# A tuned attention and adapter kernel with another beginning: bias factors made from the bias rows, products of zeros, and two stores on ScalarE's queue

## The chip, the core and the metric

The kernel runs on one core of a Trainium2 chip. The core has five engines with queues of their own: TensorE (PE; its weight loads are listed as PEld), VectorE (DVE), ScalarE (ACT), GpSimd (POOL) and SyncE (SP), which here only issues transfers. ScalarE can issue transfers too. Sixteen DMA engines carry the transfers of all queues. The metric is the device time of one execution in microseconds (us); lower is better.

## The reference: what is computed

The first half is attention with a relative position bias, for 8 batch entries, 8 heads, 576 positions and a head size of 64. The second half takes the attention output as 4608 rows of 512 and adds a mixture of 8 adapters of rank 16, of which each row uses the best two.

```
scores = q k^T / 8 + bias_table[bucket(|i - j|)]        (32 buckets)
attn   = softmax(scores);  x = attn v                   (rows: 4608 x 512)
logits = x w_gate;  the two best experts, weights w by softmax
out    = x + sum over the two of w * ((x A[e]) B[e])
```

From a distance of 128 on all positions share the last bucket. A constant in the scores drops out of the softmax, so the kernel subtracts that last bucket from the table, and the bias is zero outside a band of 128 positions on both sides.

## The kernel before, in words

**Units.** The work is cut into 32 units: a batch entry and a pair of heads (`hp`, 4 per entry). Of the 576 positions the first 512 are the main part and the last 64 the tail. A unit's main scores are computed in four groups of keys (`keys`, L416), each for 2 heads and 512 queries, and ScalarE takes the exponential of each group out of PSUM (L431, 128x1024). `edges` (L481) computes main keys against tail queries and tail keys against main queries, with one exponential (L494, 128x1024), and `corners` and `corners_first` compute tail against tail. `values` (L540) multiplies the probabilities by the values, and `normalise` divides. The second half of the kernel (gates, adapters, output) runs some units behind, spread over the same loop.

**The order of the work.** Nothing is scheduled automatically: each engine's queue runs in the order in which the code is written. Per unit `u` the loop (from L775) issues the loads of unit `u + 4` (L781), the edges, two groups of keys, the first half of the values of unit `u - 1`, two groups of keys, a turn (transposes by TensorE and a copy by VectorE, L354) that brings the q and k of unit `u + 2` into the layout that the scores need, and the second half of the values. Some turns also take the tail of a batch entry (`tl_item`, L385): that of entry 2 in unit 5. POOL casts q, k, v and the tails to bf16 a unit or two ahead (`prep`, `prep_late`), and the adapter weights in unit 4 (`weights_cast`, L273). There are three PSUM buffers for scores, used in turn, and two for everything small.

**Loads.** Nearly all transfers are issued by SP in one order, and eight may be under way: each waits for the one eight places before it, besides the cast that frees its buffer. The loads of q, k, v of unit 3 follow the start's own (L667 on); the tail's q and k are one 64-row transfer each (`load_tail`, L116), which for entry 0 are already split into two pairs of heads and two pairs of heads (L163 and L658). The loads of unit 6, the adapter weights and the tail of entry 1's values follow in unit 2 of the loop, the tail of entry 2 in unit 3.

**The bias in the main scores.** The 8 rows of the bias by distance, `gx`, are put in two interleaved halves into `gp` (L194, L195), written to a DRAM scratch `gd` (L651), and read back so that each of 64 partitions gets the row shifted by one (`table`, L205): `Wt`. A product with a reversed identity then adds the band to the scores in PSUM (L427). `Wt` comes in four transfers: for each head of the pairs, the first two pairs of heads (L206) and later the last two.

**The bias on the edges and corners** is a factor on the probabilities instead. ScalarE takes the exponential of the rows (`ge`, L655), mirrored by VectorE first (L654); the result goes to a second scratch (L657) and comes back shifted as `Wn` (`table_n`, L209, two transfers). 48 small products (`factors_l`, L216) and 16 more (`factors_t`, L236) turn pieces of it into the factors `EL`, `EC` and `ET`, and VectorE and POOL multiply the edge probabilities by them (`edge_l`, L496; `edge_t`, L501; `corners_bias`, L476).

**Products of zeros.** `keep_busy(n)` (L643) issues `n` products of 128x128 by 128x512 zeros into a PSUM buffer that nobody reads. Before, there is one call with 9, ahead of the first turn (L678).

**The end.** The last nine tiles of output rows are finished by TensorE and copied out of PSUM by ScalarE or VectorE (`out_x`, L835); each copy is followed by its store, on SP's queue. A main tile is one store of 256 KB (L309), a tail tile two of 128 KB (L331).

Of the kernel before, what the change touches and what calls it, by code (L numbers as in the profile page):

```python
# [38 lines left out]
def kernel(  # L39
# [11 lines left out]
    nc = tc.nc  # L51
# [123 lines left out]
    gp = cp.tile([H, 2, GP], BF16, tag="gp")  # L175
    nc.vector.memset(gp, 0.0)
    nc.vector.memset(tvs[0], 0.0)
    for i in range(2):
        nc.gpsimd.memset(pcs[i], 0.0)
    bts = cp.tile([H, NB], FP32, tag="bts")  # L180
# [22 lines left out]
    ET = cp.tile([128, HP, 2, 128], BF16, tag="ET")  # L203

    def table(h, g0, g1, eng):  # L205
        eng.dma_start(out=Wt[h * 64:h * 64 + 64, g0:g1, :WN],  # L206
                      in_=_dram(gd, (2 * g0 + h) * 2 * GP, [[1, 64], [4 * GP, g1 - g0], [1, WN]]))

    def table_n(h, eng):  # L209
        eng.dma_start(out=Wn[h * 64:h * 64 + 64, :, :193],  # L210
                      in_=_dram(gnd, h * GL + C - 127, [[2, 64], [2 * GL, HP], [1, 193]]))
# [4 lines left out]
    def factors_l():  # L216
        n = HP * 64
        ps = [mp.tile([128, 512], FP32, name="fl", tag="mm") for _ in range(2)]
        for hp in range(HP):
            for e in range(2):  # L220
                for h in range(2):
                    rows = slice(h * 64, h * 64 + 64)
                    for f in range(2):
                        nc.tensor.matmul(ps[h][f * 64:f * 64 + 64, hp * 64 + e * 32:hp * 64 + e * 32 + 32],
                                         lhsT=Wn[rows, hp, 129 - e:193 - e],
# [3 lines left out]
                                     lhsT=Wn[rows, hp, 1 - e:65 - e], rhs=turned(h)[:, :32],  # L229
# [6 lines left out]
    def factors_t():  # L236
        ps = [mp.tile([128, 512], FP32, name="ft", tag="mm") for _ in range(2)]
        for hp in range(HP):
            for e in range(2):
                for h in range(2):  # L240
                    rows = slice(h * 64, h * 64 + 64)
                    o = (2 * hp + e) * 64
                    nc.tensor.matmul(ps[h][64:, o:o + 64], lhsT=turned(h), rhs=Wn[rows, hp, 129 - e:193 - e],
# [4 lines left out]
    def presets():  # L248
        nc.gpsimd.memset(tvs[1], 0.0)
# [44 lines left out]
    def main_tile(b, j, f):  # L294
# [13 lines left out]
        def store(ot):  # L308
            nc.sync.dma_start(out=out[b * S:b * S + SM, :].rearrange("(p c) n -> p c n", c=4)[:, j + 2 * f, :],  # L309
                              in_=ot)  # L310
# [3 lines left out]
    def tail_tile(b):  # L314
# [14 lines left out]
        def store(ot, engs=(nc.sync, nc.sync)):  # L329
            for o in range(2):  # L330
                engs[o].dma_start(out=out[(b - 1 + o) * S + SM:(b + o) * S, :],  # L331
                                  in_=ot[64 * o:64 * o + 64, :])
# [321 lines left out]
    nc.vector.tensor_copy(gx[:, C - FAR + 1:C], _ap(gx, C + FAR - 1, [[-1, FAR - 1]]))  # L654
    nc.scalar.activation(ge[:, 128:448], gx[:, 128:448], ACT.Exp, scale=scale)  # L655
# [383 lines left out]
```

## Time and profile before

| what | value |
|---|---|
| median of 3 runs | 196.99 us (196.67 to 197.87) |
| the profiled execution | 198.93 us, of which the profile's span is 197.0 us |
| TensorE busy | 178.4 us (91% of the span) |
| ScalarE busy | 165.6 us (84%) |
| VectorE, POOL busy | 134.6 us (68%), 120.9 us (61%) |
| moved by DMA | 40.65 MB, 206 GB/s over the span |

The span is what the trace covers, from its first to its last event; all positions in time below count from its start. The profile was taken of one execution, which took 198.93 us; the median of the runs without it is 196.99. A row of a timeline reads: start, length, engine, line, operation, output<-inputs, shape, count, and in brackets how long the engine stood idle before and what released it. SPq and ACTq rows are the issuing of transfers, not the transfers themselves. A row that merges several instructions ("x4") gives the stretch from the first start to the last end.

### The profile page before, as it was taken

How to read it: one execution, taken by the hardware profiler on the slowest of the kernel's cores; microseconds unless marked ns; L12 is line 12 of the kernel's file. 1: busy time of each engine (PE TensorE's matmuls, PEld its weight loads, DVE VectorE, ACT ScalarE, POOL GpSimd, SP SyncE). 2: the span in 40 equal slices, each digit the busy share in tenths (PEclk: the TensorE clock that was granted, in tenths of full speed). 3: DMA queues.
4: the chain of work that ended last, by engine and by line, in shares of the span. 5: the costliest groups of instructions: out<-in, count | busy, mean ns of one | idle time of the engine just before them, and what ended most of it. 6: DMA issues, size and time to landing. Idle time of an engine off the chain costs nothing.

```text
span 197.0 us, 9952 instructions
## 1 busy us (share of the span) xinstructions
PE 178.4 (91%) x4272; PEld 130.2 (66%) x4272; DVE 134.6 (68%) x340; ACT 165.6 (84%) x210; POOL 120.9 (61%) x292
## 2 busy tenths in 40 slices
PE   7497998986999999999999999998999999999860
PEld 2244666664777777777677777775777777788740
DVE  6644564454467777777877768778777787788760
ACT  3459679974899999999999999998999999999670
POOL 5543656496394959495949586776859493734410
PEclk9958699997899999999999999999999999999996
DMA  5757978998977788978888967887879851114066
GB/s 137 230 149 198 277 192 239 233 208 248 269 179 227 240 235 231 283 248 216 206 253 261 275 150 219 257 269 166 236 217 315 245 180 57 57 58 108 5 242 237
DMA packets 68483, 40.65 MB, mean 206 GB/s; under 512 B 22216, under 2 KB 63704, under 8 KB 68440
## 3 DMA queue, kind: packets, MB, share of 16 engines
q1 hardware_dynamic: 67896, 39.76, 71.4%
q8 instruction: 33, 0.54, 1.3%
q10 hardware_dynamic: 544, 0.26, 0.5%
q14 instruction: 10, 0.08, 0.2%
HBM read 30.56 MB, written 9.45 MB: 203 GB/s over the span
## 4 chain that ended last, share of the span: by engine, by line
PE 52%; ACT 18%; DMA 10%; issue 6%; DVE 5%; SPq 4%; POOL 1%; POOLq 0%; ACTq 0%
ACT pk L431 14%; PE pv L518 11%; PE tx L370 8%; PE sc L422 6%; PE sc L427 4%; PE sc L492 3%; PE sc L489 3%; ACT pt L494 3%; DMA Bf<-in_moe_B_dram 3%; DMA qkt<-in_k_dram 3%; PE pv L535 2%; PE pv L526 2%; PE pv L565 2%; PE dl L614 2%; DMA vs<-in_v_dram 2%
## 5 line engine op out<-in xcount | busy, mean ns | idle before, releaser
L431 ACT ACTIVATE pk<-sc 128x1024 bf16<-128x1024 f32 x120 | 113.9, 1033 | 6.1 <-PE sc L427 6.1
L422 PE MATMUL sc<-tx 64*64 64x512 bf16 x480 | 50.5, 400 | 0.0
L427 PE MATMUL sc<-Wt,anti 64*64 64x256 bf16 (+1 forms) x480 | 43.4, 317 | 0.4 <-DMA Wt<-g_d 0.3
L518 PEld LDWEIGHTS <-pk 128*128 128x128 bf16 x1024 | 38.0, 98 | 8.5 <-issue 1.7
L518 PE MATMUL pv<-v,pk 128*128 128x65 bf16 x992 | 42.1, 195 | 0.7 <-DVE xn L558 0.7
L372 DVE COPY tx<-tx 128x2048 bf16<-128x2048 bf16 (+7 forms) x35 | 35.2, 1007 | 9.4 <-PE tx L370 7.4
L494 ACT ACTIVATE pt<-sc 128x1024 bf16<-128x1024 f32 x32 | 32.8, 1025 | 8.4 <-PE sc L492 6.4
L558 DVE TENSOR_TENSOR xn<-pv,rc 128x320 bf16<-128x320 f32 x62 | 30.5, 492 | 2.1
L581 POOL TENSOR_TENSOR a<-z,top 128x16 f32<-128x16 f32 (+2 forms) x15 | 3.3, 221 | 39.1 <-DVE top L571 37.2
L557 DVE RECIPROCAL rc<-pv 128x5 f32<-128x5 f32 x62 | 11.9, 193 | 21.5 <-PE pv L565 13.0
L303 DVE TENSOR_TENSOR ot<-dl,xn 128x512 f32<-128x512 f32 x24 | 16.6, 690 | 11.0 <-PE dl L614 11.0
L422 PEld LDWEIGHTS <-tx 64*64 64x64 bf16 x480 | 16.1, 108 | 10.2 <-issue 1.6
L136 POOL CAST v<-vs 128x512 bf16<-128x512 f32 x32 | 20.1, 629 | 3.7 <-DMA vs<-in_v_dram 3.0
L140 POOL CAST qn<-qs 128x512 bf16<-128x512 f32 x29 | 17.7, 610 | 3.9 <-DMA qs<-in_q_dram 3.5
L427 PEld LDWEIGHTS <-anti 64*64 64x64 bf16 x480 | 18.6, 109 | 1.3 <-issue 1.1
L140 POOL CAST kn<-ks 128x512 bf16<-128x512 f32 x29 | 17.8, 613 | 0.8 <-DMA ks<-in_k_dram 0.8
L535 PE MATMUL pv<-v,pt 128*128 128x65 bf16 x248 | 17.8, 195 | 0.0
L526 PE MATMUL pv<-vb,pt 128*128 128x130 bf16 x124 | 17.6, 225 | 0.0
L499 POOL TENSOR_TENSOR pt<-pt,EL 128x128 bf16<-128x128 bf16 x32 | 13.8, 430 | 5.9 <-ACT pk L431 5.9
L370 PEld LDWEIGHTS <-qn 64*128 64x128 bf16 x256 | 7.5, 95 | 12.0 <-issue 5.4
L535 PEld LDWEIGHTS <-pt 128*128 128x128 bf16 x256 | 14.2, 99 | 0.0
L504 DVE TENSOR_TENSOR pt<-pt,ET 128x256 bf16<-128x256 bf16 x32 | 12.5, 394 | 0.1
(141 smaller groups left out, 304.0 us busy)
## 6 DMA issues: line engine op xcount, KB each, us to landing
qs<-in_q_dram SPq DMA_DIRECT2D x32, 256.0 KB, 4.3
vs<-in_v_dram SPq DMA_DIRECT2D x64, 128.0 KB, 3.9
out_dram<-ot SPq DMA_DIRECT2D x32, 256.0 KB, 3.7
ks<-in_k_dram SPq DMA_DIRECT2D x62, 128.0 KB, 4.1
vt<-in_v_dram SPq DMA_DIRECT2D x16, 128.0 KB, 4.6
out_dram<-ot SPq DMA_DIRECT2D x8, 128.0 KB, 2.8
qkt<-in_q_dram SPq DMA_DIRECT2D x7, 128.0 KB, 5.3
qkt<-in_k_dram SPq DMA_DIRECT2D x7, 128.0 KB, 5.3
```

Source lines behind the costliest of these rows:

```text
L136: eng.tensor_copy(t[:, :, :, :D].rearrange("p c h d -> p h c d"), s)
L140: copy(t.rearrange("p c h d -> p h c d"), s)
L370: nc.tensor.transpose(ps[:, a, cols], src(i, a), ident[rows, rows])
L372: copy(sb[:, :n], ps.rearrange("p a (c i) -> p c a i", i=64)[:, :n])
L422: nc.tensor.matmul(sc[prt, h, :], lhsT=kT[rows, c * 128 + f * 64:c * 128 + f * 64 + 64], rhs=qT[rows, :], start=True, stop=False, skip_gro ...
L427: nc.tensor.matmul(_ap(sc[prt, h, :], p0, [[256, 2], [128, 2], [1, n]]), lhsT=turned(h), rhs=_ap(Wt[rows, hp, :], 2 * y0 + (GP if e else 1 ...
L431: nc.scalar.activation(probs[u][0][:, c, :, :], sc, ACT.Exp, scale=scale)
L494: nc.scalar.activation(probs[u][1][:, 64:], sc.rearrange("p h x -> p (h x)"), ACT.Exp, scale=scale)
L518: nc.tensor.matmul(pv[:, o:o + W1], lhsT=pk_slice(u, c, h, j + 2 * f), rhs=vm[:, c, h, :], start=first, stop=False, skip_group_check=True)
L526: nc.tensor.matmul(_ap(pv, h * W1, [[130, 2], [1, W1]]), lhsT=probs[u][1][:, x0:x0 + 128], rhs=tvs[b % 2][:, 2 * hp + h].rearrange("p f d ...
L535: nc.tensor.matmul(pv[:, o:o + W1], lhsT=probs[u][1][:, x0:x0 + 128], rhs=vts[u % NV][:, c, h, :], start=False, stop=False, skip_group_che ...
L558: nc.vector.tensor_tensor(xs[b][:, j, hp], _ap(pv, 0, [[W1, 5], [1, D]]), _ap(rc, 6 * j, [[1, 5], [0, D]]), op=ALU.mult)
```

## The change

It does the following; all line numbers above are those of the kernel before.

- `Wt` comes in two transfers of 64 rows, each for all four pairs of heads. The later two transfers for the last two pairs are gone.
- The mirrored copy of `gx`, the exponential `ge`, its store to a second scratch and the two loads of `Wn` are gone. Instead ScalarE takes two exponentials of pieces of `Wt` (`near_rows`, 128x272 each) into a `Wn` of another layout, and the factor products take their rows from it (`table_row`).
- Products of zeros are added behind the first turn (4), behind the second turn (4), behind the edges of unit 1 (5) and behind the third turn (3).
- The corner scores and their exponential and the edges of unit 2 stand ahead of the first keys. On ScalarE's queue the corner exponential, the edge exponential of unit 2 and the two `near_rows` come ahead of all key exponentials. `factors_l` stands behind two groups of keys instead of four, `factors_t` behind four groups instead of five.
- POOL multiplies the corner factors ahead of the casts of the first values. Its presets stand ahead of the cast of unit 1's q. The memset of `tvs[1]` moves from the presets to the start, and VectorE's memset of `ET` from behind the second turn to the start, ahead of the bias rows.
- At the end the tile `(L - 1, 3)` comes before `(L, 4)` instead of after it. Its store, and the second half of the store of `(L, 4)`, are issued by ScalarE.

The split of the tail loads is the same in both kernels.

```diff
     gp = cp.tile([H, 2, GP], BF16, tag="gp")
+    ET = cp.tile([128, HP, 2, 128], BF16, tag="ET")
     nc.vector.memset(gp, 0.0)
     nc.vector.memset(tvs[0], 0.0)
+    nc.vector.memset(ET[:64], 1.0)
     for i in range(2):
         nc.gpsimd.memset(pcs[i], 0.0)
+    nc.gpsimd.memset(tvs[1], 0.0)
...
-    ge = cp.tile([H, GL], BF16, tag="ge")
-    gnd = nc.dram_tensor("gn_d", (H, GL), BF16, kind="Internal").ap()
-    Wn = cp.tile([128, HP, 194], BF16, tag="Wn")
...
-    def table(h, g0, g1, eng):
-        eng.dma_start(out=Wt[h * 64:h * 64 + 64, g0:g1, :WN],
-                      in_=_dram(gd, (2 * g0 + h) * 2 * GP, [[1, 64], [4 * GP, g1 - g0], [1, WN]]))
-
-    def table_n(h, eng):
-        eng.dma_start(out=Wn[h * 64:h * 64 + 64, :, :193],
-                      in_=_dram(gnd, h * GL + C - 127, [[2, 64], [2 * GL, HP], [1, 193]]))
+    Wn = cp.tile([128, 2, HP, 68], BF16, tag="Wn")
+
+    def near_rows(i):
+        nc.scalar.activation(Wn[:, i].rearrange("p g (x two) -> p g x two", two=2),
+                             _ap(Wt, 128 - 64 * i, [[WN + 1, HP], [1, 34], [GP, 2]]), ACT.Exp, scale=scale)
+
+    def table(h):
+        nc.sync.dma_start(out=Wt[h * 64:h * 64 + 64, :, :WN],
+                          in_=_dram(gd, 2 * h * GP, [[1, 64], [4 * GP, HP], [1, WN]]))
+
+    def table_row(rows, hp, y):
+        i = 0 if y >= 256 else 1
+        return Wn[rows, i, hp, y - 256 + 128 * i:y - 192 + 128 * i]
...
-                                         lhsT=Wn[rows, hp, 129 - e:193 - e],
+                                         lhsT=table_row(rows, hp, 258 - e),
...
     def presets():
-        nc.gpsimd.memset(tvs[1], 0.0)
...
-        def store(ot, engs=(nc.sync, nc.sync)):
+        def store(ot, eng=nc.sync):
             for o in range(2):
-                engs[o].dma_start(out=out[(b - 1 + o) * S + SM:(b + o) * S, :],
-                                  in_=ot[64 * o:64 * o + 64, :])
+                (nc.sync, eng)[o].dma_start(out=out[(b - 1 + o) * S + SM:(b + o) * S, :],
+                                            in_=ot[64 * o:64 * o + 64, :])
...
-    nc.vector.tensor_copy(gx[:, C - FAR + 1:C], _ap(gx, C + FAR - 1, [[-1, FAR - 1]]))
-    nc.scalar.activation(ge[:, 128:448], gx[:, 128:448], ACT.Exp, scale=scale)
     load(2, "k")
-    nc.sync.dma_start(out=gnd[:, 128:448], in_=ge[:, 128:448])
     load_tail(0, "qk", 2)
     for h in range(2):
-        table(h, 0, 2, nc.sync)
-    for h in range(2):
-        table_n(h, nc.sync)
+        table(h)
     load(0, "v")
     load_tail(0, "v")
-    for h in range(2):
-        table(h, 2, HP, nc.sync)
     load(3, "qk")
...
+    presets()
     cast(1, "q", nc.gpsimd)
     cast_half(1, "k", 0, nc.scalar)
     keep_busy(9)
     turn([qk_item(0), tl_item(0, 0, 2)])
+    keep_busy(4)
     cast_half(1, "k", 1, nc.vector)
-    presets()
...
     edges(0)
     turn([qk_item(1)])
+    keep_busy(4)
     edges(1)
     cast(2, "q", nc.vector)
-    nc.vector.memset(ET[:64], 1.0)
+    keep_busy(5)
     turn([qk_item(2), tl_item(0, 2, HP)])
+    keep_busy(3)
+    px = corners_first(0)
+    edges(2)
+    near_rows(0)
+    near_rows(1)
     keys(0, KO[0])
     keys(0, KO[1])
-    edges(2)
+    factors_l()
     keys(0, KO[2])
-    keys(0, KO[3])
-    factors_l()
     edge_l(0)
+    corners_bias(0, px)
     cast(0, "v", nc.gpsimd)
     cast_tail(0, "v", nc.gpsimd)
+    keys(0, KO[3])
+    factors_t()
     keys(1, KO[0])
-    factors_t()
     edge_t(0)
     keys(1, KO[1])
-    px = corners_first(0)
-    corners_bias(0, px)
     edge_l(1)
...
-    def out_x(t, dl, xin=True, copy=act):
+    def out_x(t, dl, xin=True, copy=act, eng=nc.sync):
...
-        t.store(ot)
+        t.store(ot, eng)
...
-    out_x(T(L, 4), fin(0, 1), True, dve)
-    out_x(T(L - 1, 3), fin(2, 0))
+    out_x(T(L - 1, 3), fin(2, 0), eng=nc.scalar)
+    out_x(T(L, 4), fin(0, 1), True, dve, nc.scalar)
```

More of the change, by code (lines that the diff above doesn't have):

```diff
@@ L228, in factors_l @@
                     nc.tensor.matmul(_ap(ps[h][rows], n + hp * 64 + e, [[2, 32]]),
-                                     lhsT=Wn[rows, hp, 1 - e:65 - e], rhs=turned(h)[:, :32],
+                                     lhsT=table_row(rows, hp, 130 - e), rhs=turned(h)[:, :32],
                                      start=False, stop=True, skip_group_check=True)
@@ L242, in factors_t @@
                     o = (2 * hp + e) * 64
-                    nc.tensor.matmul(ps[h][64:, o:o + 64], lhsT=turned(h), rhs=Wn[rows, hp, 129 - e:193 - e],
+                    nc.tensor.matmul(ps[h][64:, o:o + 64], lhsT=turned(h), rhs=table_row(rows, hp, 258 - e),
                                      start=(hp == 0 and e == 0), stop=True, skip_group_check=True)
@@ L306, in add @@
                                     op=ALU.add)
-        def store(ot):
-            nc.sync.dma_start(out=out[b * S:b * S + SM, :].rearrange("(p c) n -> p c n", c=4)[:, j + 2 * f, :],
+        def store(ot, eng=nc.sync):
+            eng.dma_start(out=out[b * S:b * S + SM, :].rearrange("(p c) n -> p c n", c=4)[:, j + 2 * f, :],
                               in_=ot)
```

2 lines of the change are left out of this document (1 added, 1 removed).

## The prediction

> **What bounds the kernel now.** I read the page first, then the chain of work that ended last, then the timeline of each engine around the places where the chain leaves TensorE and ScalarE, and last TensorE's granted clock by windows.
>
> ```profile
> PE 178.4 (91%) x4272; PEld 130.2 (66%) x4272; DVE 134.6 (68%) x340; ACT 165.6 (84%) x210; POOL 120.9 (61%) x292
> ```
>
> TensorE and ScalarE share the bound: in the middle each unit (one batch entry and pair of heads) costs some 5.1 us of both. The change does not touch that middle. What it can move is the beginning, up to where a steady pace sets in, and the last stores. The edge exponentials (`L494`), one per unit, show where the beginning ends:
>
> ```profile
> 39.49 1.02 ACT L494 ACTIVATE pt<-sc 128x1024 bf16<-128x1024 f32 x1 [0.19 <-issue]
> 48.54 1.02 ACT L494 ACTIVATE pt<-sc 128x1024 bf16<-128x1024 f32 x1 [0.47 <-PE sc L492]
> 54.15 1.02 ACT L494 ACTIVATE pt<-sc 128x1024 bf16<-128x1024 f32 x1
> 59.23 1.02 ACT L494 ACTIVATE pt<-sc 128x1024 bf16<-128x1024 f32 x1 [0.40 <-PE sc L492]
> ```
>
> From 39.49 to 48.54 are 9.05 us, and from 48.54 to 54.15 are 5.61, where the next takes 5.08. So unit 5 loses 4.0 us and unit 6 loses 0.5. Who is late there:
>
> ```profile
> 45.71 0.29 PE L370 MATMUL tx<-ident,qkb 64*128 64x64 bf16 x8 [1.57 <-POOL qkb L148]
> ```
> ```profile
> 38.07 0.61 POOL L274 CAST A<-A4f 128x512 bf16<-128x512 f32 x1 [2.03 <-DMA A4f<-in_moe_A_dram]
> 45.04 0.61 POOL L148 CAST qkb<-qkt 128x512 bf16<-128x512 f32 x1 [0.52 <-DMA qkt<-in_k_dram]
> ```
> ```profile
> 39.91 5.01 DMA qkt<-in_k_dram
> ```
>
> TensorE stands 1.57 us before it can turn the tail of batch 2. POOL cast that tail only at 45.04, because the load, issued at 39.91, landed at 44.92. POOL had waited for a transfer at 38.07 as well. So up to here the stream of loads on SP's queue runs late against the compute, and what brings that stream forward is worth time; what merely starts the exponentials earlier is not, unless the loads follow. The stall has a second price, the clock:
>
> ```profile
> 6.13:9.55 3.42, 1.27 (x32) 0.77 (x32) 2.61 (x5) 1.83 (x3) 2.49 (x12) 1.00 0.74 217
> 9.55:12.96 3.41, 2.67 (x42) 1.51 (x46) 2.42 (x4) 1.02 (x1) 2.42 (x5) 0.51 0.57 142
> 12.96:16.37 3.41, 3.41 (x67) 1.89 (x61) 0.00 (x0) 3.10 (x4) 0.00 (x0) 0.50 0.59 150
> 16.37:19.79 3.42, 1.95 (x77) 1.14 (x74) 2.39 (x6) 3.03 (x4) 1.64 (x4) 0.99 0.87 225
> 40.26:43.67 3.41, 2.99 (x59) 2.28 (x56) 1.53 (x5) 2.25 (x4) 3.26 (x7) 1.00 0.95 195
> 43.67:47.08 3.41, 1.76 (x61) 1.40 (x55) 1.87 (x5) 1.78 (x2) 2.69 (x5) 1.00 0.91 237
> 47.08:50.50 3.42, 3.06 (x46) 2.01 (x47) 0.99 (x3) 2.23 (x4) 1.22 (x2) 0.51 0.82 243
> ```
>
> The columns after the window's length are the busy time of PE, PEld, DVE, ACT, POOL, then the clock and the DMA engines' share. The clock changes only at multiples of 3.41 us. It falls to half behind windows in which TensorE was busy for 37% (1.27 of 3.42), 57% and 52%, and rises behind one that was full. The half clock from 47.08 is the echo of the 1.57 us stall, and I charge it the 0.5 us that unit 6 loses.
>
> **SP's queue.** The change takes out the store of `ge`, both loads of `Wn` and the second pair of `Wt` loads; the first pair now brings all pairs of heads.
>
> ```profile
> 8.92 1.23 SPq L206 DMA_DIRECT2D Wt<-g_d  x2
> 10.20 1.26 SPq L210 DMA_DIRECT2D Wn<-gn_d  x2
> 11.50 1.12 SPq L109 DMA_DIRECT2D vs<-in_v_dram  x2
> 12.66 2.24 SPq L122 DMA_DIRECT2D vt<-in_v_dram  x2
> 14.95 1.28 SPq L206 DMA_DIRECT2D Wt<-g_d  x2
> 16.27 0.59 SPq L112 DMA_DIRECT2D qs<-in_q_dram  x1
> ```
>
> The two removed pairs occupied SP for 1.26 + 1.28 = 2.54 us ahead of the loads of unit 3, which move from 16.27 to some 13.75. Every later load stands behind them. The rest of the list is the same, and each issue waits for the transfer eight places earlier, as before, so the lead of 2.5 us lasts unless a buffer comes free late (the casts that free them were done some us ahead, and only the casts of units 0 and 1 move) or the DMA engines saturate. Their share between 9.55 and 16.37 was 0.57 and 0.59, so there is room for it there. From below, the lead is what the engines no longer carry: by bytes, `Wn`'s 193 KB at the 217 GB/s of the first window, 0.9 us. I take 2.5, since the shares in front of 16.37 are far from 1. Then the tail lands at 42.4, POOL casts it by 43.1 instead of 45.65, and its turn starts at 43.2, 2.5 us earlier, if TensorE is there by then.
>
> **Is TensorE there?** In the old run it arrived at 45.71 - 1.57 = 44.14. What the start does to that is the second term.
>
> ```profile
> 8.85 0.29 PE L370 MATMUL tx<-ident,kn 64*128 64x64 bf16 x8 [0.42 <-DVE kn L639]
> ```
> ```profile
> 1.17 4.02 PE L645 MATMUL busy<-A4f 128*128 128x512 bf16 x9 [1.17 <-DVE A4f L166]
> ```
> ```profile
> 188.41 0.22 PE f L838
> ```
> ```profile
> 11.45 0.82 DVE L372 COPY tx<-tx 128x1280 bf16<-128x1280 bf16 x1
> ```
> ```profile
> 13.27 1.94 ACT L431 ACTIVATE pk<-sc 128x1024 bf16<-128x1024 f32 x2 [1.51 <-PE sc L427]
> 20.19 0.38 ACT L473 ACTIVATE pcx<-cn 128x256 bf16<-128x256 f32 x1
> 23.16 1.94 ACT L431 ACTIVATE pk<-sc 128x1024 bf16<-128x1024 f32 x2 [1.37 <-PE sc L427]
> ```
>
> A product of zeros costs 4.02 / 9 = 0.45 at the cold clock and 0.22 warm, the issue step of an equally large product at the end. Sixteen are added: 4 ahead of the edges of unit 0, where TensorE waits for a copy anyway (0.88 us warm, hidden), then 4, 5 and 3 in its path. Warm, the path is: 9.14 (8.85 + 0.29), four zeros to 10.0, edges of unit 1 to 10.5 (half a us, an estimate from the eight transposes' 0.29), five zeros to 11.6, the third turn to 12.2, DVE's copy of 0.82 to 13.1 (three zeros beside it, free), corner scores 0.3 and edges of unit 2 to 13.9, ScalarE's corner exponential (0.38) beside them, edge exponential (1.02) to 15.0, two `near_rows` of 128x272 at about 0.42 each, from the 0.38 of 128x256, to 15.8. Then key exponentials every 0.97 (1.94 / 2): the first at 15.8, not 13.27, but the corner and edge exponentials of the old 13.27 to 23.16 are behind it, and so is the old 1.37 us wait if the casts that the first values need come in time. Seven of them end at 22.6, so the eighth starts 0.55 us earlier than at 23.16. Cold between 9.55 and 12.96, the second group of zeros ends at 10.45 and the third at 13.2, and the eighth starts at about 24.1, 0.9 late.
>
> Which? In the window from 6.13 TensorE would now be busy 1.27 + 0.88 for the first zeros + 0.4 for the second ones, 2.55 of 3.42, 75%: between the 57% that lost the clock and the 88% (2.99) that kept it. I hold both equally likely; from 12.96 on the clock is warm either way, since the window before it is full. The Trainium skill (TensorE: Matmul & The Clock Gate, Part 1: The HAM clock gate) says that the clock drops after an idle window of about 3.4 us and that the window is free-running, so that its phase varies between runs. By that rule a partly busy window would never cost the clock, the zeros would bring nothing after the first warm-up, and the early end would hold; the drops behind windows of 37% to 57% here speak against it, and the measurement decides.
>
> POOL's wait at 38.07 goes too, and with it a wait of TensorE for POOL's corner product:
>
> ```profile
> 42.50 0.20 PE L537 MATMUL pv<-vb,pc 128*128 128x65 bf16 x1 [0.36 <-POOL pc L478]
> ```
>
> TensorE is then ready for the tail at 44.14 - 0.36 - 0.55 = 43.2 (warm) or at 44.14 - 0.36 + 0.9 = 44.7 (cold). The gain is 45.71 less that, 2.5 or 1.0; the tail itself, ready at 43.2, allows no more than 2.5. I take the middle, 1.8, as I hold both clocks equally likely. With the stall gone, the 0.5 us of half clock behind it go as well (0 to 0.5, taken 0.5, since the window would be fuller than any here that lost the clock).
>
> **The small edits.** The `Wt` transfers become 256 rows each. The nearest row for such a one is that of `Wn`, also 256 rows:
>
> ```profile
> DMA to landing us min/median/max: 4.2/4.2/4.2
> ```
>
> The second, issued at about 9.55, lands at 13.75; ScalarE needs it at 15.0, TensorE at 13.9, so it costs nothing. If ScalarE were free earlier it would be the next wait. The memset of `ET` moves in front of the bias chain on DVE:
>
> ```profile
> 3.23 0.23 DVE L181 TENSOR_SCALAR bts<-btT 8x32 f32<-8x32 f32 x1 [0.48 <-DMA btT<-in_bias_table_dram]
> 4.63 0.21 DVE L195 COPY gp<-gx 8x128 bf16<-8x128 bf16 x1
> 5.36 0.30 SPq L651 DMA_DIRECT2D g_d<-gp  x1
> 10.40 0.91 DVE L695 MEMSET ET<- 64x1024 bf16 x1 [0.16 <-issue]
> ```
>
> It costs 0.91 - 0.48 = 0.43 of that chain, and `gp` was ready 0.52 before SP took it (5.36 - 4.84): free, with 0.1 us to spare; without that cover 0.43 would be added to everything behind `Wt`. POOL's memsets only change places.
>
> **The last stores.** Two of them move to ScalarE's queue.
>
> ```profile
> 193.00:193.50 0.50, 0.00 (x0) 0.00 (x0) 0.00 (x0) 0.00 (x0) 0.00 (x0) 1.00 1.03 381
> 194.00:194.50 0.50, 0.00 (x0) 0.00 (x0) 0.00 (x0) 0.00 (x0) 0.00 (x0) 0.50 0.93 217
> ```
> ```profile
> 192.02 1.28 SPq L331 DMA_DIRECT2D out_dram<-ot  x2
> 193.40 0.54 SPq L309 DMA_DIRECT2D out_dram<-ot  x1
> ```
>
> SP's last issue ends at 193.94 and would end at about 192.65, 1.3 us earlier. But the engines are full (1.03), so the bytes do not go faster; only the dip to 217 GB/s can be filled, 0.5 x (1 - 217 / 381) = 0.2 us. Ends 0 and 1.3, taken 0.2.
>
> **Sum.** 1.8 + 0.5 + 0.2 = 2.5 us. The profiled execution took 198.93 (its span of 197.0 and 1.93 around it), and the median of the runs is 196.99, 1% below it. I take the gain over unchanged: a span of 194.5, and a median of 196.99 - 2.5 = 194.5.
>
> **The rivals.** *The DMA engines are the limit, not SP's issue.* For it: their share of 0.91 to 0.95 from 40.26 on. Against it: 0.57 to 0.59 ahead of the loads that move. The lead is then 0.9 us, the stall shrinks by 0.9, the half clock stays, and with 0.2 at the end the time is 195.9.
>
> *The zeros hold up the start (the other side).* If the clock stays halved, all zeros cost 0.45: the first group ends at 8.6 instead of 7.6, the 4 and 5 cost 4.05 instead of 2.0, and the turn, copy, corner and edge products double too. The eighth key exponential then starts at 26.2 or later, 3 to 5 us late. It decides from 45.71 - 44.14 = 1.57 us on, for so much the old stall absorbs: 196.99 + (3 to 5) - 1.57 - 0.2 = 198.2 to 200.2, say 198.8. Against it: the nine zeros at the start did release the clock once, as 7 of the 16 would again.
>
> *The loads' lead and the early start both come through, and the stores gain too:* 2.5 + 0.5 and half of the 1.3 at the end, 3.65: 193.3. It needs the warm clock, and stores that the full engines somehow take faster, which the 1.03 speaks against.
>
> *POOL's casts are late next.* The casts of the first values now stand behind POOL's corner product on its queue:
>
> ```profile
> 20.70 0.97 POOL L478 TENSOR_TENSOR pc<-pcx,EC 128x256 bf16<-128x256 bf16 x1 [0.39 <-POOL vb L152]
> ```
>
> If the first value products wait for them, the cold start is late by 0.97 more, TensorE reaches the tail at 45.7 as before, and only the half clock's 0.5 is left: 196.5. Against it: the eight key exponentials ahead give POOL until 21 or so.
>
> **Chances.** The forecast 0.5, with its own range 193.9 to 195.7; DMA limit 0.15; zeros hold up 0.12; both come through 0.13; POOL's casts 0.10. Leaving out the zeros' rival above 197.3 and the tip below 192.9 makes the range 192.9 to 197.3. A measurement of this kernel tells about 1% from no change, here 195.0 and 199.0: faster by more than that 0.5 x 0.85 + 0.13 + 0.05 = 0.60; slower 0.08; within 0.32.
>
> **What would show it.** Right: the loads of unit 3 issued near 13.75, POOL's A cast without its 2.03 wait, no wait of over 0.5 us for the tail's turn near 43, a full clock at 47 to 50, about 5.1 us per unit from 39 on. Wrong: a half clock after 13, the eighth key exponential after 24, the tail landing after 44, a last store that ends the span more than half a us earlier.

## The result and the profile after

| | kernel before | changed kernel |
|---|---|---|
| median, same chip, 15 runs each | 197.52 us (196.11 to 198.81) | 196.20 us (193.85 to 198.90) |
| ratio, 95% interval | 1 | 0.9896 [0.9856, 0.9937] |
| the profiled execution; its span | 198.93; 197.0 | 198.90; 197.1 |
| the same, run again later (12 runs) | | 194.66 us, ratio 0.9909 [0.9869, 0.9949] |
| profiled execution of that; its span | | 195.15; 193.4 |

The change is worth 1.0%, about 2 us; the forecast was 194.5 / 196.99 = 0.987, inside the interval. Ratios leave out executions over 1.5% above the fastest of their kernel; by the medians of all 15 runs the gain is 1.3 us. The first profile of the changed kernel is of an execution of 198.90 us, the longest of its 15, so a second one is read beside it: the same code run again (`e9_after_again`). Lines L373, L430, L434, L476, L497, L648 of the changed kernel are the old L370, L427, L431, L473, L494, L645; L206 is `near_rows`, which is new.

The edge exponentials, changed kernel, first profile (timeline of ScalarE):

```profile
38.01 1.02 ACT L497 ACTIVATE pt<-sc 128x1024 bf16<-128x1024 f32 x1 [0.18 <-PE sc L495]
...
47.08 1.02 ACT L497 ACTIVATE pt<-sc 128x1024 bf16<-128x1024 f32 x1 [0.46 <-POOL kn L140]
...
54.02 1.02 ACT L497 ACTIVATE pt<-sc 128x1024 bf16<-128x1024 f32 x1
...
58.94 1.02 ACT L497 ACTIVATE pt<-sc 128x1024 bf16<-128x1024 f32 x1 [0.23 <-PE sc L495]
```

The same view of the second profile:

```profile
37.09 1.02 ACT L497 ACTIVATE pt<-sc 128x1024 bf16<-128x1024 f32 x1 [0.19 <-issue]
...
46.09 1.02 ACT L497 ACTIVATE pt<-sc 128x1024 bf16<-128x1024 f32 x1 [0.47 <-PE sc L495]
...
51.09 1.02 ACT L497 ACTIVATE pt<-sc 128x1024 bf16<-128x1024 f32 x1
...
56.08 1.02 ACT L497 ACTIVATE pt<-sc 128x1024 bf16<-128x1024 f32 x1 [0.31 <-PE sc L495]
```

Unit 5 began at 39.49 before; now it begins 1.48 or 2.40 us earlier. But it still takes 9.07 or 9.00 us, where it took 9.05. The gain was made ahead of unit 5, and the wait that I meant to shorten is still there. TensorE's rows, first profile and then second:

```profile
15.14 0.37 PE L430 MATMUL sc<-Wt,anti 64*64 64x256 bf16 x3 [1.62 <-DMA Wt<-g_d]
...
44.25 0.29 PE L373 MATMUL tx<-ident,qkb 64*128 64x64 bf16 x8 [2.10 <-POOL qkb L148]
```
```profile
42.99 0.36 PE L373 MATMUL tx<-ident,qkb 64*128 64x64 bf16 x8 [1.71 <-POOL qkb L148]
```

TensorE was ready for the tail of entry 2 at 44.25 - 2.10 = 42.15, or at 42.99 - 1.71 = 41.28; before it was 44.14. The tail came earlier by as much, no more. POOL's casts and the transfer behind them, first profile (timeline; a row of the chain of waits):

```profile
35.92 0.61 POOL L277 CAST A<-A4f 128x512 bf16<-128x512 f32 x1 [0.92 <-DMA A4f<-in_moe_A_dram]
...
43.58 0.61 POOL L148 CAST qkb<-qkt 128x512 bf16<-128x512 f32 x1 [0.76 <-DMA qkt<-in_k_dram]
```
```profile
38.05 5.41 DMA qkt<-in_k_dram
```

SP's queue, first and second profile:

```profile
13.39 0.62 SPq L112 DMA_DIRECT2D qs<-in_q_dram  x1
...
38.05 0.64 SPq L128 DMA_DIRECT2D qkt<-in_k_dram  x1
```
```profile
12.15 0.62 SPq L112 DMA_DIRECT2D qs<-in_q_dram  x1
...
36.95 0.63 SPq L128 DMA_DIRECT2D qkt<-in_k_dram  x1
```

The loads of unit 3 go out 2.88 or 4.12 us earlier than at 16.27, the tail's k load 1.86 or 2.96 earlier than at 39.91. On the way 1.0 to 1.2 us of the lead is lost. The DMA engines' share between 12.96 and 16.37, which was 0.59 before, is now 1.16 and 1.22 in the two profiles, with 229 and 251 GB/s instead of 150.

The start itself, on ScalarE, first and second profile:

```profile
15.12 0.82 ACT L206 ACTIVATE Wn<-Wt 128x272 bf16<-128x272 bf16 x2 [0.85 <-DMA Wt<-g_d]
15.85 9.41 ACT L434 ACTIVATE pk<-sc 128x1024 bf16<-128x1024 f32 x10
```
```profile
14.21 0.81 ACT L206 ACTIVATE Wn<-Wt 128x272 bf16<-128x272 bf16 x2
14.92 9.42 ACT L434 ACTIVATE pk<-sc 128x1024 bf16<-128x1024 f32 x10
```

Ten key exponentials now follow one another without a gap. The eighth starts at 15.85 + 7 x 0.94 = 22.4, or at 14.92 + 7 x 0.94 = 21.5, instead of 23.16. In the first profile the second `Wt` transfer, issued about 9.4, had landed only by 15.1; ScalarE lost 0.85 us and TensorE 1.62.

TensorE's clock, first profile (windows: PE, PEld, DVE, ACT, POOL busy, then clock, DMA share, GB/s); the first two rows have the bounds used for the kernel before, the others those at which the clock of this execution changed:

```profile
6.13:9.55 3.42, 3.07 (x46) 1.45 (x48) 2.37 (x5) 1.43 (x2) 0.94 (x5) 1.00 0.85 238
9.55:12.96 3.41, 3.41 (x60) 1.68 (x63) 0.89 (x2) 1.21 (x2) 2.19 (x5) 1.00 0.78 155
...
38.52:41.93 3.41, 3.35 (x77) 2.64 (x74) 1.84 (x7) 2.79 (x4) 3.03 (x6) 1.00 1.10 215
41.93:45.34 3.41, 1.31 (x52) 1.14 (x47) 1.05 (x3) 1.49 (x2) 2.59 (x5) 1.00 0.88 221
45.34:48.75 3.41, 3.02 (x47) 1.80 (x45) 1.27 (x3) 1.95 (x3) 1.31 (x3) 0.50 0.84 234
48.75:52.16 3.41, 3.41 (x55) 2.32 (x54) 1.25 (x5) 2.09 (x3) 0.51 (x3) 0.50 0.92 279
52.16:55.58 3.42, 3.42 (x99) 2.81 (x94) 1.64 (x3) 2.97 (x6) 2.64 (x8) 1.00 0.91 192
```

The zeros kept the clock full at the start (3.07 us busy in the first row). The stall around 43 left TensorE busy for 1.31 of 3.41 us, and two windows at half clock followed. In the second profile it was one, and it lay elsewhere:

```profile
39.64:43.05 3.41, 1.70 (x44) 1.03 (x42) 1.36 (x5) 2.25 (x3) 2.36 (x5) 1.00 0.76 194
43.05:46.46 3.41, 3.41 (x65) 2.77 (x69) 1.91 (x3) 0.65 (x2) 2.28 (x4) 0.50 0.67 199
46.46:49.87 3.41, 3.39 (x92) 2.51 (x85) 1.57 (x6) 3.41 (x5) 0.42 (x3) 1.00 0.89 261
```

The Trainium skill (TensorE: Matmul & The Clock Gate, Part 1: The HAM clock gate) says that the window is free-running, so that its phase differs between runs. The traces agree: the edges lie at 45.34 and 52.16 in one execution and at 43.05 and 46.46 in the other. The window need not be idle for the clock to drop: 38% and 50% busy were too little in these two.

The end of the first profile (windows):

```profile
193.00:193.50 0.50, 0.00 (x0) 0.00 (x0) 0.00 (x0) 0.00 (x0) 0.00 (x0) 1.00 1.01 369
...
194.50:195.00 0.50, 0.00 (x0) 0.00 (x0) 0.00 (x0) 0.00 (x0) 0.00 (x0) 1.00 0.82 176
```

The engines are as full as before, and the dip (176 GB/s) is still there. SP's last issue ended at 192.87 instead of 193.94, but the end did not move with it. From the last edge exponential to the end of the span took 197.0 - 174.69 = 22.3 us before, and 197.1 - 174.41 = 22.7 now.

### The profile page after: what moved, and what is told of

Its sections match the earlier page's. It is cut to its first block, busy times and chain, and to the rows that moved or that the text cites. A ratio compares the mean times of both kernels' runs of the same rounds, so it can differ in the third digit from the quotient of the medians.

```text
span 197.1 us, 9979 instructions
## 1 busy us (share of the span) xinstructions
PE 178.5 (91%) x4288; PEld 130.2 (66%) x4288; DVE 133.9 (68%) x339; ACT 165.6 (84%) x211; POOL 121.3 (62%) x292
## 4 chain that ended last, share of the span: by engine, by line
PE 48%; ACT 15%; DMA 13%; DVE 7%; issue 6%; POOL 4%; SPq 3%; POOLq 0%; DVEq 0%; ACTq 0%
ACT pk L434 12%; PE pv L521 11%; PE tx L373 8%; PE sc L425 6%; DMA vs<-in_v_dram 4%; PE sc L430 3%; PE sc L495 3%; DMA qkt<-in_k_dram 3%; PE sc L492 3%; DMA qs<-in_q_dram 3%; DMA A4f<-in_moe_A_dram 2%; ACT pt L497 2%; PE pv L538 2%; PE pv L529 2%; PE pv L568 2%
## 5 line engine op out<-in xcount | busy, mean ns | idle before, releaser
L434 ACT ACTIVATE pk<-sc 128x1024 bf16<-128x1024 f32 x120 | 113.4, 1036 | 2.8 <-PE sc L430 2.7
L425 PE MATMUL sc<-tx 64*64 64x512 bf16 x480 | 49.3, 391 | 0.2 <-ACT pk L434 0.2
L430 PE MATMUL sc<-Wt,anti 64*64 64x256 bf16 (+1 forms) x480 | 42.4, 311 | 1.6 <-DMA Wt<-g_d 1.6
L497 ACT ACTIVATE pt<-sc 128x1024 bf16<-128x1024 f32 x32 | 32.8, 1024 | 7.3 <-PE sc L495 5.4
L306 DVE TENSOR_TENSOR ot<-dl,xn 128x512 f32<-128x512 f32 x24 | 16.6, 690 | 11.1 <-PE dl L617 10.6
L430 PEld LDWEIGHTS <-anti 64*64 64x64 bf16 x480 | 18.4, 107 | 2.3 <-issue 2.0
L373 PEld LDWEIGHTS <-qn 64*128 64x128 bf16 x256 | 7.5, 94 | 12.7 <-issue 6.3
```

The source lines that it names most:

```text
L373: nc.tensor.transpose(ps[:, a, cols], src(i, a), ident[rows, rows])
L425: nc.tensor.matmul(sc[prt, h, :], lhsT=kT[rows, c * 128 + f * 64:c * 128 + f * 64 + 64], rhs=qT[rows, :], start=True, stop=False, skip_gro ...
L430: nc.tensor.matmul(_ap(sc[prt, h, :], p0, [[256, 2], [128, 2], [1, n]]), lhsT=turned(h), rhs=_ap(Wt[rows, hp, :], 2 * y0 + (GP if e else 1 ...
L434: nc.scalar.activation(probs[u][0][:, c, :, :], sc, ACT.Exp, scale=scale)
L497: nc.scalar.activation(probs[u][1][:, 64:], sc.rearrange("p h x -> p (h x)"), ACT.Exp, scale=scale)
```

## The experiments

Theory S: the lead of the load stream on SP's queue is the gain. Theory Z: the compact start on TensorE and ScalarE is. All kernels in one table, in us, of each one's profiled execution. "Tail wait" is TensorE's wait for the tail of entry 2; "units 5 to 7" runs from the edge exponential of unit 5 to that of unit 8. Waits and positions are those of one execution each, and several of these took longer than the median of their kernel (`e2_early_tail` 197.76 against 195.76, `e7_late_adapter_B` 196.09 against 194.39).

| kernel | unit 3 starts | unit 5 starts | tail wait | units 5 to 7 | ratio to before, 95% interval |
|---|---|---|---|---|---|
| before | 29.06 | 39.49 | 1.57 | 19.74 | 1 |
| after | 27.68 | 38.01 | 2.10 | 20.93 | 0.9896 [0.9856, 0.9937] |
| e9_after_again | 26.76 | 37.09 | 1.71 | 18.99 | 0.9909 [0.9869, 0.9949] |
| e1_no_zeros | 26.98 | 37.31 | 0.69 | 17.29 | 0.9894 [0.9856, 0.9932] |
| e2_early_tail | 26.87 | 37.21 | 1.03 | 20.35 | 0.9942 [0.9907, 0.9978] |
| e3_stores_on_sp | 28.18 | 38.52 | none | 16.58 | 0.9870 [0.9824, 0.9916] |
| e4_spare_loads | 28.86 | 40.54 | 0.47 | 17.07 | 1.0017 [0.9980, 1.0054] |
| e6_loads_alone | 33.27 | 43.61 | none | 16.57 | 1.0126 [1.0076, 1.0176] |
| e7_late_adapter_B | 26.76 | 37.09 | 1.66 | 20.11 | 0.9894 [0.9840, 0.9948] |
| e8_before_late_B | 29.03 | 39.36 | 0.50 | 17.39 | 0.9972 [0.9931, 1.0014] |
| e10_no_zeros_sp | 26.82 | 37.16 | 1.27 | 19.09 | 0.9898 [0.9853, 0.9943] |
| e11_turn_later | 26.68 | 37.01 | 2.12, in unit 6 | 21.40 | 0.9972 [0.9937, 1.0007] |
| e12_before_turn_later | 29.35 | 39.69 | 2.28, in unit 6 | 19.94 | 1.0097 [1.0059, 1.0135] |
| e13_turn_later_cast_stays | 27.88 | 38.21 | none | 16.41 | 0.9835 [0.9783, 0.9887] |

**The changed kernel without its sixteen products of zeros.**

```diff
-    keep_busy(4)
...
-    keep_busy(4)
...
-    keep_busy(5)
...
-    keep_busy(3)
```

> The changed kernel without the sixteen added products of zeros. Theory S (the gain is the lead of the load stream on SP's queue): the loads stay where they are, the second pair of edge exponentials starts as early as before, and the ratio to the kernel before stays at 0.990, give or take 0.004. Theory Z (the gain is the start on TensorE and ScalarE, held up by a full clock): the clock falls to half from about 9.5 to 16 us, the eighth key exponential starts 1 us or more later than 22.4, and the ratio goes to 0.996 to 1.000.

Measured: 0.9894 [0.9856, 0.9932], not to be told from the changed kernel. Its clock did fall at the start (windows):

```profile
6.13:9.55 3.42, 1.38 (x32) 0.84 (x32) 1.89 (x5) 1.43 (x2) 1.13 (x5) 0.81 0.84 234
9.55:12.96 3.41, 2.66 (x56) 1.92 (x58) 1.21 (x3) 1.41 (x2) 1.99 (x5) 0.50 1.02 214
12.96:16.37 3.41, 3.20 (x79) 2.22 (x73) 0.51 (x2) 3.34 (x5) 0.00 (x0) 0.50 1.16 248
```

So the zeros keep the clock, and that is worth nothing that shows in the ratio: at half clock without them unit 3 starts at 26.98, at full clock with them at 26.76 and 27.68. At this place ScalarE is all but full (3.34 of 3.41 us busy in the last row), and TensorE's work at half clock (3.20) still goes on beside it.

**The tail's q and k ahead of the adapter weights.**

```diff
         if u == 2:
+            load_tail(2, "qk")
             weights_load()
...
         if u in tload:
-            load_tail(tload[u])
+            load_tail(tload[u], "v" if tload[u] == 2 else "qkv")
```

> The changed kernel with the q and k loads of the tail of batch 2 moved ahead of the adapter weights, in unit 2 instead of unit 3. Theory S: unit 5's 2.10 us wait for that tail (lands at 43.46) goes, the clock stays full from 45 to 52, and the time falls by 2 to 3 us against the changed kernel: ratio 0.975 to 0.981. Rival: the DMA engines are full from 38 to 42 and another load, the adapter weights or unit 7's k, is late in its place: the wait moves, and the ratio is 0.986 to 0.991.

Measured: 0.9942 [0.9907, 0.9978], no better than without it; the intervals overlap. In the profile the tail had landed in time, but POOL waited for the adapter weights, which now came later, and for the tail of entry 1's values (1.54 us), and so cast the tail of entry 2 late (POOL, then TensorE):

```profile
35.56 0.61 POOL L277 CAST A<-A4f 128x512 bf16<-128x512 f32 x1 [1.87 <-DMA A4f<-in_moe_A_dram]
```
```profile
43.88 0.29 PE L373 MATMUL tx<-ident,qkb 64*128 64x64 bf16 x8 [1.03 <-POOL qkb L148]
```

Swapping two loads here only swapped who waits.

**All last stores back on SP, in the old order.**

```diff
-    out_x(T(L - 1, 3), fin(2, 0), eng=nc.scalar)
-    out_x(T(L, 4), fin(0, 1), True, dve, nc.scalar)
+    out_x(T(L, 4), fin(0, 1), True, dve)
+    out_x(T(L - 1, 3), fin(2, 0))
```

> The changed kernel with the last two tiles in the old order and all stores issued by SP. If the stores on ScalarE's queue bring the 0.2 us of the forecast: ratio 0.991, not to be told from 0.990. If the rate of the DMA engines sets the end and two queues disturb each other (the profile of the changed kernel ends 0.1 us later though its last copy is ready 0.2 us earlier): 0.5 us faster, 0.987. If SP's issue was the bound: 1.3 us slower, 0.996.

Measured: 0.987 [0.9824, 0.9916], 6 runs; from the last edge exponential (169.82) to the end of the span (192.2) 22.4 us, against 22.7. All profiles agree on it: in the five with two stores on ScalarE's queue this stretch takes 22.6 to 22.7 us, in the nine with all stores on SP 22.3 to 22.4. So the new order of the last two tiles, with its stores, gains nothing and costs about 0.3 us. The execution profiled here happened to have the tail in time:

```profile
42.45 0.28 PE L373 MATMUL tx<-ident,qkb 64*128 64x64 bf16 x8
```

**Four spare loads where the late `Wt` pair was.** They put the lead of the load stream back to nothing, with the compact start unchanged. The spare loads are read by nobody. They move 4 x 112.2 = 449 KB, where the change took out 198 KB (2 x 96.5 of `Wn`, 5 of `ge`'s store).

```diff
     load_tail(0, "v")
+    for h in range(2):
+        spare(h, 0)
+    for h in range(2):
+        spare(h, 2)
     load(3, "qk")
```

> The changed kernel with four spare loads of 64 rows for two pairs of heads each (the size of the old bias loads) into a tile that nobody reads, at the place of the old last pair. They cost SP 2.5 us and the DMA engines about 450 KB ahead of unit 3's loads. Theory S: the lead of the load stream is gone and with it the gain, ratio 0.998 to 1.004. Theory Z: the start on TensorE and ScalarE is as before, ratio 0.990 to 0.993.

Measured: 1.0017 [0.998, 1.0054]; the gain is gone. SP's queue, POOL and ScalarE:

```profile
12.52 3.57 SPq L215 DMA_DIRECT2D Wx<-g_d  x4
16.14 0.59 SPq L112 DMA_DIRECT2D qs<-in_q_dram  x1
```
```profile
25.30 0.62 POOL L136 CAST v<-vs 128x512 bf16<-128x512 f32 x1 [2.37 <-DMA vs<-in_v_dram]
```
```profile
28.86 1.02 ACT L502 ACTIVATE pt<-sc 128x1024 bf16<-128x1024 f32 x1 [1.59 <-issue]
```

With unit 3's loads at 16.14, about where they were before (16.27), POOL waits 2.37 us for the values and ScalarE 1.59 at unit 3, which starts at 28.86, as before. A compact start whose loads come late is given back within 15 us; unit 5 starts at 40.54, even 1.05 later than before. So the start alone is not the gain. Whether it is the place in the queue or the bytes that counts is not shown, since the spare loads put back both, and 251 KB more than the change took out.

**The short bias path in the old order.** The new bias path and its shorter queue (unit 3's loads go out at 12.37), but keys, edges, corners and factors in the old order (`near_rows` right ahead of `factors_l`, behind four key exponentials and the edge exponential of unit 2), no zeros, stores on SP.

```diff
-    keep_busy(3)
-    px = corners_first(0)
+    keys(0, KO[0])
+    keys(0, KO[1])
     edges(2)
+    keys(0, KO[2])
+    keys(0, KO[3])
     near_rows(0)
     near_rows(1)
-    keys(0, KO[0])
-    keys(0, KO[1])
     factors_l()
-    keys(0, KO[2])
     edge_l(0)
-    corners_bias(0, px)
...
-    keys(0, KO[3])
-    factors_t()
     keys(1, KO[0])
+    factors_t()
     edge_t(0)
     keys(1, KO[1])
+    px = corners_first(0)
+    corners_bias(0, px)
```

> The part of the change that shortens the queue, alone: bias rows in two transfers, factors from near_rows, but the old order of keys, edges, factors and corners, no added products of zeros, and all stores on SP in the old order. Theory S (the lead of the loads is the gain): ratio to the kernel before 0.985 to 0.990, as the changed kernel without zeros or stores. Theory Z (the compact start is needed as well): 0.994 to 0.998, with the two near_rows on ScalarE in front of the fifth key exponential costing 0.8 us.

Measured: 1.0126 [1.0076, 1.0176], slower than before. Theory S, that the shorter queue brings the gain in whatever order, falls here. ScalarE:

```profile
18.69 0.84 ACT L206 ACTIVATE Wn<-Wt 128x272 bf16<-128x272 bf16 x2
21.44 1.02 ACT L434 ACTIVATE pk<-sc 128x1024 bf16<-128x1024 f32 x1 [1.90 <-PE sc L430]
...
27.19 1.94 ACT L434 ACTIVATE pk<-sc 128x1024 bf16<-128x1024 f32 x2 [1.37 <-PE sc L430]
...
33.27 1.02 ACT L497 ACTIVATE pt<-sc 128x1024 bf16<-128x1024 f32 x1
```

The factor products need `near_rows`, and in the old order those stand behind four key exponentials on ScalarE; TensorE waits for them, ScalarE then waits 1.90 us for TensorE. `Wt` for all pairs also lands later: TensorE waited 0.94 and 0.74 us for it, and the first key exponential starts at 14.15 instead of 13.27. With these gaps TensorE's clock is at half in every window from 9.55 to 26.61. The eighth key exponential starts at 27.19 instead of 23.16, unit 3 at 33.27 instead of 29.06. Part of the 4.2 us comes back later: with everything loaded in time, units 5 to 7 take 16.57 us instead of 19.74. So moving the exponential from the eight rows of `ge` to the 128 partitions of `Wt` makes it a step of ScalarE in the start's path, and the new order is needed with it: the same kernel in the new order (`e10_no_zeros_sp`, below) has a ratio of 0.9898. A lead without that step in the path was not run, so what the lead alone would bring is open.

**A 256 KB load of adapter weights later.** `moe_B` is loaded in unit 4 and cast in unit 6, once in the changed kernel without zeros and with stores on SP, once in the kernel before with nothing else changed.

```diff
-        nc.sync.dma_start(out=Bf, in_=moe_B.rearrange("e r d -> (e r) d"))
...
-        nc.gpsimd.tensor_copy(Bc, Bf)
...
+        if u == 4:
+            nc.sync.dma_start(out=Bf, in_=moe_B.rearrange("e r d -> (e r) d"))
...
+        if u == 6:
+            nc.gpsimd.tensor_copy(Bc, Bf)
```

> The changed kernel without the added zeros, all stores on SP in the old order, and the 256 KB load of the adapters' B moved from unit 2 to unit 4 (its cast to unit 6), since it is first needed in unit 8. Theory S: every load of units 7 and 8 and the tail of batch 2 come another 1 us earlier, no wait for the tail in unit 5 in any run and the clock never halves behind it: ratio 0.978 to 0.984 and a narrower spread of runs. Rival: the stall is already gone in most runs without zeros and extra stores, or the DMA engines and not the place in the queue set the time of the tail: 0.986 to 0.990.

> The kernel before with only that move of the load of B. Nothing of the change is in it. Theory S: 1 us of lead takes most of the 1.57 us wait for the tail away and in part of the runs the half clock behind it: ratio 0.991 to 0.995. Theory Z (the start is what counts) or a wait that moves to the next load: 0.998 to 1.000.

Measured: 0.9894 [0.984, 0.9948] and 0.9972 [0.9931, 1.0014]. The first is where it was without the move (0.9898 [0.9853, 0.9943], below), with a wait of 1.66 us still there in the longest of its six executions, and the second can't be told from 1. In the profile of the second the wait did shrink, and units 5 to 7 took 17.39 instead of 19.74:

```profile
43.96 0.29 PE L368 MATMUL tx<-ident,qkb 64*128 64x64 bf16 x8 [0.50 <-POOL qkb L148]
```

Its median of 196.44 us is nevertheless only 0.3 below that of the kernel before on the same chip (196.75). One profile shows one execution's wait, and the wait differs between executions.

**The changed kernel again.**

> The changed kernel once more, on the same chip as the other three: ratio 0.990, give or take 0.004. A profile of a quicker execution should show unit 5's wait for the tail short or absent and a full clock from 45 to 52; if the wait is as long as in the first profile (2.10 us) and the execution is still 3 us quicker, the wait is not what spreads the runs.

Measured: 0.9909 [0.9869, 0.9949]; its profile is the second one above.

**Without zeros and with stores on SP.**

> The changed kernel without its sixteen products of zeros and with all last stores back on SP: the short bias path and the compact order alone. Theory S (the lead of the loads, kept by the compact order, is the whole gain) expects what the runs without one or the other gave, 0.987 to 0.990 of the kernel before, some 194.5 us. The rival, that zeros and stores on ScalarE each carry a part which the other covered, expects 0.993 or more.

Measured: 0.9898 [0.9853, 0.9943], and a wait of 1.27 us for the tail. Within that interval the short path and the new order, in which POOL's and VectorE's moved operations are included, are the whole effect, and zeros and stores are no part of it.

**The tail's turn a unit later,** to take TensorE's wait away: in the kernel of the run before (no zeros, stores on SP), and in the kernel before the change.

```diff
-    tturn = {3 if c == 1 else 5 if c == 2 else 4 * c - 4: c for c in range(1, B)}
+    tturn = {3 if c == 1 else 6 if c == 2 else 4 * c - 4: c for c in range(1, B)}
...
-    tcorner = {max(4 * c - 3, 3) + i: (c, 2 * i) for c in range(1, B) for i in range(2)}
+    tcorner = {max(4 * c - 3, 3) + (c == 2) + i: (c, 2 * i) for c in range(1, B) for i in range(2)}
```

> The same kernel, and the tail of batch entry 2 is cast and turned in unit 6 instead of unit 5, so that TensorE cannot wait for its load in unit 5. If that wait is where the rest of the lead is lost, unit 5 takes 6.6 to 7.1 us in each execution, unit 6 takes 5.1, and the median falls below the kernel without the move by what the wait still costs on average: 0.5 to 1.5 us, to a ratio of 0.980 to 0.985. The rival, that the transfers themselves are the limit there, expects another load to be waited for (adapter weights, or the q and k of unit 6 or 7), and a ratio within 0.3% of the kernel without the move.

> The kernel before, changed only in that the tail of batch entry 2 is cast and turned in unit 6 instead of unit 5. It takes away the wait of 1.57 us and the half clock behind it, with nothing of the new beginning. If the gain of the change is the shortening of that wait, this edit alone brings about the same: 1.6 to 2.1 us, a ratio of 0.990 to 0.992. The rival: the gain of the change is made ahead of unit 5, or the transfers are the limit, and this edit alone brings less than 0.6 us (0.997 or more).

Measured: 0.9972 [0.9937, 1.0007] and 1.0097 [1.0059, 1.0135], the first 0.7% above the kernel without the move, with intervals that barely overlap, the second slower than the kernel before. Unit 5 got short (6.71 and 5.66 us), but the wait moved to unit 6. POOL and TensorE of the first:

```profile
49.10 0.61 POOL L148 CAST qkb<-qkt 128x512 bf16<-128x512 f32 x1
```
```profile
49.77 0.29 PE L373 MATMUL tx<-ident,qkb 64*128 64x64 bf16 x8 [2.12 <-POOL qkb L148]
```

The cast no longer waits for a transfer (no bracket in POOL's row); it stands last on POOL's queue, behind unit 6's gate operations and casts. I had moved the cast along with the turn, and so made a new wait. These two runs say nothing on the price of the old one. The next edit leaves the cast in unit 5 and moves only the turn:

```diff
-    tq = {w if c == 2 else w - 1: c for w, c in tturn.items()}
+    tq = {w - 1: c for w, c in tturn.items()}
```

> As the kernel with the tail's turn in unit 6 (no zeros, stores on SP), but POOL casts the tail of batch entry 2 in unit 5 again, where it stood; only TensorE's turn is a unit later. With cast and turn both in unit 6 the cast came last on POOL's queue (49.10) and TensorE waited 2.12 us for it there. If what is left of the lead is lost to the order of that one cast and turn, neither unit 5 nor unit 6 now waits for the tail: unit 5 takes 6.6 to 7.1 us, unit 6 takes 5.1 to 5.9, and the ratio is 0.980 to 0.986. The rival, that the transfers set the pace between 37 and 47 us, expects POOL to wait at the next casts instead (q and k of unit 7 or the values' tails), TensorE or ScalarE to wait for those in unit 5 or 6, and a ratio of 0.988 to 0.994.

Measured: 0.9835 [0.9783, 0.9887], median 193.47 (193.12 to 195.37, 6 runs), the lowest ratio of all; its interval overlaps with that of the version without the move (0.9898 [0.9853, 0.9943]). POOL, then TensorE:

```profile
43.67 0.61 POOL L148 CAST qkb<-qkt 128x512 bf16<-128x512 f32 x1 [1.04 <-DMA qkt<-in_k_dram]
```
```profile
42.03 0.28 PE L373 MATMUL tx<-ident,kn 64*128 64x64 bf16 x8
42.15 0.28 PE L373 MATMUL tx<-ident,xn 64*128 64x64 bf16 x8
...
47.09 0.28 PE L373 MATMUL tx<-ident,qkb 64*128 64x64 bf16 x8
```

Here too the tail came late: POOL waits 1.04 us for it and casts it at 43.67, when the turn of unit 5 was over. But nobody waits for POOL, TensorE goes on at 42.15 and turns the tail at 47.09, the clock stays full, and units 5 to 7 take 16.41 us. In this execution nothing of the lead is lost behind unit 5; that the move is worth more than the version without it is likely, but the intervals do not show it.

## Why the prediction was right, and where it was not

The time came out on the forecast's side and about as large (1.0% for 1.3%), but by another way than the sum. That the totals are so near is in part luck: the stall that was to go stayed, and the start gained more than the sum gave it. The spans of two profiled executions of the same code lie 0.1 us above and 3.6 below that of the kernel before.

- *The lead on SP's queue (2.5 us): right at its start.* It was 2.88 and 4.12 at unit 3 and 1.86 and 2.96 at the tail. The sum counted the issue of the two pairs that went; in the second profile `Wt` also went out at 8.37 instead of 8.92, and the two loads of the values' tails took 1.29 us of the queue instead of 2.24. That it "lasts" was wrong by 1.0 to 1.2 us. The tail was to land at 42.4; it landed at 38.05 + 5.41 = 43.46 in the first profile, and in the second its turn came at 42.99, where I said 43.2. POOL's A cast, which was to lose its wait of 2.03, kept 0.92 and 0.81 of it.
- *TensorE ready at 43.2 to 44.7: the step that failed.* It was ready at 42.15 and 41.28. The wait of 0.36 us for POOL's corner product went, as forecast. The 0.55 us of the start was mis-sized. In the old start two waits stood behind the eighth key exponential that I had not counted (ScalarE, kernel before):

```profile
25.36 1.02 ACT L431 ACTIVATE pk<-sc 128x1024 bf16<-128x1024 f32 x1 [0.26 <-PE sc L427]
...
29.06 1.02 ACT L494 ACTIVATE pt<-sc 128x1024 bf16<-128x1024 f32 x1 [0.39 <-POOL v L136]
```

  Both are gone: 0.65 us. And in the second profile the first key exponential starts at 14.92, not at the 15.8 of my sum, and they follow every 0.94 us, not 0.97; the eighth starts at 21.5 where I had 22.6. Together 1.65 + 0.65 = 2.30 us, which is 29.06 - 26.76. In the first profile the late `Wt` took 0.9 of that back.
- *So the wait did not go.* TensorE came earlier by as much as the tail. "Gain 1.8 at the wait" was in fact 1.48 to 2.40 us ahead of unit 5, passed on unchanged. The tail's turn came 1.46 and 2.72 us earlier because the tail did, not because TensorE was ready. "No wait of over 0.5 near 43" was wrong (2.10, 1.71), and "full clock at 47 to 50" wrong in the first profile (0.50).
- *The half clock (0.5 us): mis-sized.* I charged the old stall 1.57 + 0.5. Without a wait units 5 to 7 take 16.4 to 16.6 us in three profiles; with one of 0.5 to 0.7 in unit 5, 17.1 to 17.4; with 1.0 to 1.7, 19.0 to 20.4; with 2.1, 20.9. The step between them is the clock: it fell to half behind the wait in all eight profiles with 1.0 us or more, and stayed full in all six with 0.7 or less. So, against 16.58 of `e3_stores_on_sp`, the stall with its echo cost 19.74 - 16.58 = 3.2 us in the profile before. The forecast took the part in unit 6 for the whole echo and left out that of unit 5. Unit 5 takes 6.6 us even without a wait, so 2.4 of the 4.0 us that the forecast called lost were the stall's, 0.9 of them beyond the wait of 1.57. (e2's 20.35 holds a second wait, for the adapter weights.)
- *The zeros: warm, as in one of the two ends, but free for another reason.* The clock held; without zeros it did not, and the time was the same. The clock at the start is not in the path, so the two ends of that term, 2.5 and 1.0, rested on a question that does not matter here.
- *`Wt` "costs nothing": wrong at times.* I took 4.2 us from issue to landing, from `Wn`, which has as many rows but 96.5 KB where `Wt` now has 224.5; it was 3.9 to 4.4 in the second profile, and up to 5.7 in the first, and ScalarE and TensorE both waited.
- *The stores (0.2): wrong, 0.3 us worse.* SP's last issue did end earlier, by 1.07 us for the 1.3 forecast, and it did not matter. The full engines (1.03) were the row to go by; the dip was not filled.
- *The rival that the DMA engines are the limit* was partly true: their share rose to 1.16 and 1.22 where I had counted on the room of 0.59, the lead shrank on its way to unit 5, and giving the tail precedence made the adapter weights late. That the zeros hold up the start, or that POOL's casts do, did not come about.

What stays open: why the same code has the tail in time in one execution and 2 us late in another. The k load of the tail took 5.41 us in the first profile, at a DMA share of 1.10, and the runs of the changed kernel spread over 5 us. Whether a typical execution of the kernel before loses the whole 3.2 us in units 5 to 7 is not shown either: its profiled execution was 1.4 us above the median, and a kernel that took most of the wait away in its profile gained only 0.3 us in its median (196.44 to 196.75).

## What to carry to other kernels

Where loads and compute race to one meeting point, look at both: here the short path in the old order made the kernel slower, the early start with its loads put back gave nothing, and both together moved the meeting earlier, with the wait still in it. Price a stall of TensorE with its echo at half clock, by comparing whole stretches with and without the wait; here 1.57 us of waiting stood for 3.2. When a cast waits for a late load, try to leave the cast where it is and move its consumer: moving both put the cast at the end of a queue here.

## What the runs showed of the hardware

A window of 3.41 us in which TensorE was busy for 1.31 or 1.70 us was followed by half clock, and one of 3.02 busy at half clock did not end it; the next, of 3.41, did. In the profile before, one of 3.06 of 3.42 at half clock (from 47.08) was enough to end it. Waits of 0.5 to 0.7 us in unit 5 left the clock full and cost about their own length in units 5 to 7; with waits of 1.0 to 2.1 us there it fell to half, and they cost 2.4 to 4.4. The two `Wt` transfers, in the same place of the same code, took 3.9 to 4.4 us to land in one execution and 4.1 to 5.7 in another.
